# Weighting v in 16-bit with heads innermost: a ScalarE copy of v, a strided kv product, and a new instruction order in a fused attention and MLP kernel

## The chip, the cores and the metric

The kernel runs on one core of one Trainium2 chip. The metric is the device time of one execution in microseconds (us), median over runs. In the text PE is TensorE, ACT is ScalarE, DVE is VectorE, POOL is GpSimd, and SP is the engine that issues most DMA. SBUF and PSUM are the core's two on-chip memories; in this kernel PE's products land in PSUM, in banks of 512 32-bit columns. The granted clock is the share of its full clock that PE had, as the profile records it. "Span" is the length of the one profiled execution, some 2 us shorter than its time. "L773" is line 773 of that kernel's file; the same source statement has other line numbers in other kernels.

## The reference, cut to what matters

A pre-norm block: a layer norm, linear attention with a softmax feature map, then a second norm and a wide MLP (2048 tokens, 576 channels, 32 heads of 18, 4608 hidden).

```
q, k, v = split(layernorm(x) @ wqkv)            # 32 heads of 18
pk = einsum("bhsd,hdf->bhsf", k, w_phi)         # the same for q
phi_k = concat([softmax(pk), softmax(-pk)])
kv  = einsum("bhsf,bhsd->bhfd", phi_k, v)       # sum over the 2048 tokens
z   = sum of phi_k over tokens
o   = (phi_q . kv) / (phi_q . z)
h   = x + o @ wo
out = h + mlp(layernorm(layernorm(h)))
```

## The kernel before: the parts that matter here

The first 78 us (attention, first phase) walk over 16 tiles of 128 tokens. For tile t the kernel does K (PE: fused k projection; ACT: two exponentials), R (DVE: sums over each head's 18 features and their reciprocal), V (PE: v projection into PSUM banks 2 and 3), M (DVE: v times the reciprocal softmax sums, for both signs), and G (PE: the kv products of the exponentials with the weighted v, added up over the tiles). Q units (q projection with exponentials) fill PE where there is room. The v of a tile stays in PSUM until M has read it, because there is one pair of v banks.

```
def vx(t):                                   # weighted v: sign, head, value (value innermost)
    return vext[t % 2].rearrange("p (s h d) -> p s h d", s=2, h=H)

# M: 32-bit v out of PSUM times the 16-bit weight, broadcast over the 18 values
P.add("dve", lambda e: e.tensor_tensor(
    vx(t)[:, :, :, 0:DH],
    ps_all[:, 512 * VB:512 * VB + D].rearrange("p (h d) -> p h d", h=H).unsqueeze(1)
    .to_broadcast([128, 2, H, DH]),
    vx(t)[:, :, :, DH:DH + 1].to_broadcast([128, 2, H, DH]), ALU.mult), ...)

# G: for both signs and five groups of 7, 7, 7, 4, 7 heads
e.matmul(ps_all[:, col:col + 19 * nh], Ek[eb][:, ...],
         vext[vb][:, 608 * s + 19 * h0:608 * s + 19 * (h0 + nh)], ...)   # neighbouring columns

# kvr: after the last tile, kv out of PSUM times a 0/1 mask, two DVE operations
kvr[:, :, 0:25, 0:19] = ps_kv(512 * 5, [[512, 2], [19, 25], [1, 19]]) * mask25
kvr[:, :, 25:32, 0:19] = ps_kv(512 * 7, [[133, 2], [19, 7], [1, 19]]) * mask7
...
```

Every engine's instruction order is a list written out in the kernel (`PLAN`), one label per piece of work: K3, V2, M1, and so on. After kvr come the numerators N (PE) for the first two tiles, a serial chain over DVE, PE and POOL, and then the MLP, from about 95 us to the end.

The softmax here doesn't subtract the row's maximum and nothing guards it: scores larger than these inputs give would overflow.

## Time and profile before

| | before |
|---|---|
| time, median of 3 runs | 411.02 us |
| span | 408.5 us |
| first k projection starts | 11.79 us |
| first numerator product starts (PE timeline) | 77.80 us |
| first MLP product starts (PE timeline) | 95.18 us |
| PE busy from 13 to 78 us (windows) | 63.02 of 65.0 us |

The busy-time row of the page, and the first row of the chain that ended last (shares of the span by engine):

```profile
PE 398.3 (97%) x5000; PEld 288.5 (71%) x5000; DVE 180.7 (44%) x450; ACT 182.4 (45%) x422; POOL 93.7 (23%) x129
...
PE 87%; DMA 4%; DVE 4%; POOL 2%; ACT 1%; issue 1%; SPq 0%; DVEq 0%; POOLq 0%
```

PE bounds the kernel. The groups that the change touches, from 13 to 78 us (columns: line, engine, operation, output<-input, shapes, count | busy us, mean ns of one | idle time of the engine just before them and who ended it):

```profile
L786 DVE TENSOR_TENSOR RB<-ps_all,RB 128x1152 bf16<-128x1152 f32 x16 | 21.4, 1345 | 3.9 <-PE ps_all L763 3.9
L753 ACT ACTIVATE RB<-ps_all 128x576 bf16<-128x576 f32 x32 | 19.0, 647 | 8.0 <-PE ps_all L746 6.3 <-PE ps_all L801 1.7
L801 PE MATMUL ps_all<-RB 128*128 128x133 bf16 x128 | 11.4, 222 | 0.0
L1048 DVE TENSOR_TENSOR kvr<-ps_all,OTR 128x950 bf16<-128x950 f32 x1 | 1.2, 1151 | 1.0 <-PE ps_all L801 1.0
L1052 DVE TENSOR_TENSOR kvr<-ps_all,mask 128x266 bf16<-128x266 f32 x1 | 0.4, 428 | 0.0
```

L786 is the product M: 1.345 us for 1152 elements. L753 is the exponential of a 576-column tile out of PSUM: 0.647 us. L801 is a kv product (222 ns is the length of one; they overlap, and one starts 56 ns after the other). The waits of PE from 10 to 95 us (who waited <- for whom: us in total, times, longest):

```profile
PE ps_all L746 <- ACT tpn L486: 1.1, 1, 1.1
PE ps_all L564 <- DVE obuf L920: 0.6, 1, 0.6
PE ps_all L746 <- DVE RA L605: 0.5, 1, 0.5
PE ps_all L746 <- DMA yT<-ybuf: 0.5, 1, 0.5
...
```

No row shows PE waiting for M (L786), neither in its kv products (L801) nor in its v projection (L763). DVE has work to do, but it is not what PE waits for.

### The profile page before, as it was taken

How to read it: one execution, taken by the hardware profiler on the slowest of the kernel's cores; microseconds unless marked ns; L12 is line 12 of the kernel's file. 1: busy time of each engine (PE TensorE's matmuls, PEld its weight loads, DVE VectorE, ACT ScalarE, POOL GpSimd, SP SyncE). 2: the span in 40 equal slices, each digit the busy share in tenths (PEclk: the TensorE clock that was granted, in tenths of full speed). 3: DMA queues.
4: the chain of work that ended last, by engine and by line, in shares of the span. 5: the costliest groups of instructions: out<-in, count | busy, mean ns of one | idle time of the engine just before them, and what ended most of it. 6: DMA issues, size and time to landing. Idle time of an engine off the chain costs nothing.

```text
span 408.5 us, 11674 instructions
## 1 busy us (share of the span) xinstructions
PE 398.3 (97%) x5000; PEld 288.5 (71%) x5000; DVE 180.7 (44%) x450; ACT 182.4 (45%) x422; POOL 93.7 (23%) x129
## 2 busy tenths in 40 slices
PE   7998999989999999999999999999999999999996
PEld 4565666858965896599559956985697579658853
DVE  6997999786445125422442244234325412300000
ACT  5985856668840373046205700660175026404800
POOL 5578730022203203201220022002200220111000
PEclk9999999999999999999999999999999999999999
DMA  7699242495211100111110011001100120000000
GB/s 237 117 244 308 51 101 68 152 345 174 34 34 32 33 18 18 32 33 20 33 31 18 18 34 45 19 19 32 32 18 19 30 32 19 18 14 19 2 2 29
DMA packets 45595, 25.87 MB, mean 63 GB/s; under 512 B 32744, under 2 KB 44520, under 8 KB 45544
## 3 DMA queue, kind: packets, MB, share of 16 engines
q1 hardware_dynamic: 45400, 24.99, 24.1%
q8 instruction: 39, 0.64, 0.7%
q10 hardware_dynamic: 144, 0.15, 0.1%
q14 instruction: 12, 0.10, 0.1%
HBM read 15.13 MB, written 2.36 MB: 43 GB/s over the span
## 4 chain that ended last, share of the span: by engine, by line
PE 87%; DMA 4%; DVE 4%; POOL 2%; ACT 1%; issue 1%; SPq 0%; DVEq 0%; POOLq 0%
PE ps_all L1127 35%; PE ps_all L1195 35%; PE ps_all L952 4%; PE ps_all L763 3%; PE ps_all L831 3%; PE ps_all L746 3%; PE ps_all L852 2%; DMA yT<-ybuf 2%; PE ps_all L801 2%; DMA w2a<-in_A_wqkv_dram 1%; DMA x_all<-in_A_x_dram 1%; PE ps_all L615 1%; DVE x_all L972 1%; POOL ybuf L527 1%; DVE RA L605 0%
## 5 line engine op out<-in xcount | busy, mean ns | idle before, releaser
L1138 ACT ACTIVATE RA<-ps_all,b1T 128x256 bf16<-128x256 f32 x288 | 115.0, 479 | 176.9 <-PE ps_all L1127 162.1
L1127 PE MATMUL ps_all<-yT,w1sb 64*128 64x256 bf16 x2304 | 152.2, 269 | 0.0
L1127 PEld LDWEIGHTS ps_all<-yT,w1sb 64*128 64x128 bf16 x2304 | 135.0, 94 | 6.4
L1195 PE MATMUL ps_all<-w2a,RA 128*128 128x512 bf16 (+1 forms) x640 | 96.2, 286 | 0.0
L1127 PE MATMUL ps_all<-yT,w1t 64*128 64x256 bf16 x288 | 71.5, 270 | 0.0
L1195 PEld LDWEIGHTS ps_all<-w2a,RA 128*128 128x128 bf16 x640 | 45.8, 98 | 35.6 <-ACT RA L1138 1.5
L1195 PE MATMUL ps_all<-RB,RA 128*128 128x64 bf16 (+1 forms) x512 | 67.7, 286 | 0.0
L1204 DVE TENSOR_TENSOR WQ<-ps_all,tmpo 128x64 bf16<-128x64 f32 (+1 forms) x32 | 14.7, 458 | 101.5 <-PE ps_all L1195 89.1
L1195 PEld LDWEIGHTS ps_all<-RB,RA 128*128 128x128 bf16 x512 | 33.5, 98 | 32.3
L972 DVE SCALAR_TENSOR_TENSOR x_all<-ps_all,x_all 128x576 bf16<-128x576 f32 x16 | 12.1, 758 | 82.2 <-PE ps_all L952 82.1
L920 POOL TENSOR_TENSOR obuf<-tpn 128x576 bf16<-128x576 f32 x14 | 19.6, 1401 | 86.5 <-DVE tpn L915 76.4
L984 POOL TENSOR_TENSOR st<-st,neghalf 128x1 f32<-128x1 f32 x16 | 8.8, 552 | 133.3 <-DVE st L986 133.3
L837 ACT ACTIVATE Eq<-ps_all 128x512 bf16<-128x512 f32 (+1 forms) x48 | 25.3, 526 | 14.6 <-PE ps_all L831 13.4
L1201 POOL TENSOR_TENSOR tmpo<-x_all,b2bc 128x576 f32<-128x576 bf16 x16 | 20.4, 1274 | 43.5 <-DVE WQ L1204 43.5
L952 PE MATMUL ps_all<-wo_sb,OTR 64*128 64x288 bf16 x288 | 29.7, 283 | 0.2
L1127 PEld LDWEIGHTS ps_all<-yT,w1t 64*128 64x128 bf16 x288 | 26.3, 94 | 2.2 <-DVE WQ L1204 0.3
L831 PE MATMUL ps_all<-yT,WQ 128*128 128x256 bf16 x200 | 25.2, 273 | 0.2 <-ACT Eq L837 0.2
L746 PE MATMUL ps_all<-RA,yT 128*128 128x512 bf16 (+1 forms) x160 | 22.4, 286 | 2.5 <-ACT tpn L486 1.1
L786 DVE TENSOR_TENSOR RB<-ps_all,RB 128x1152 bf16<-128x1152 f32 x16 | 21.4, 1345 | 3.9 <-PE ps_all L763 3.9
L527 POOL TENSOR_SCALAR ybuf<-x_all,st 128x576 bf16<-128x576 bf16 x10 | 22.9, 2296 | 0.6 <-POOL st L514 0.6
L753 ACT ACTIVATE RB<-ps_all 128x576 bf16<-128x576 f32 x32 | 19.0, 647 | 8.0 <-PE ps_all L746 6.3
L763 PE MATMUL ps_all<-RB,yT 128*128 128x512 bf16 (+1 forms) x160 | 22.1, 286 | 0.0
(103 smaller groups left out, 317.0 us busy)
## 6 DMA issues: line engine op xcount, KB each, us to landing
w1sb<-in_B_w_dram SPq DMA_DIRECT2D x8, 576.0 KB, 6.9
w2a<-in_B_w_dram SPq DMA_DIRECT2D x4, 720.0 KB, 6.7
RB<-in_B_w_dram SPq DMA_DIRECT2D x2, 1152.0 KB, 7.6
out_dram<-WQ SPq DMA_DIRECT2D x16, 144.0 KB, 1.8
x_all<-in_A_x_dram SPq DMA_DIRECT2D x3, 576.0 KB, 4.9
w2a<-in_A_wqkv_dram SPq DMA_DIRECT2D x2, 288.0 KB, 5.4
RB<-in_A_wqkv_dram SPq DMA_DIRECT2D x1, 576.0 KB, 5.9
wo_sb<-in_A_wo_dram SPq DMA_DIRECT2D x1, 576.0 KB, 5.3
```

The lines of the kernel that those rows point to most:

```text
L527: P.add(eng, lambda e: e.tensor_scalar(ybuf[yb][:, 0:D], src, mean, rstd, ALU.subtract, ALU.mult), reads=[r_src, *r_st], writes=[res(f"ybu ...
L746: P.add("pe", lambda e, c=c, o=o, n=n: e.matmul(ps_all[:, 512 * KB + o:512 * KB + o + n], yT[:, c, sl * 128:(sl + 1) * 128], weffk[:, c, o ...
L763: P.add("pe", lambda e, c=c, o=o, n=n: e.matmul(ps_all[:, 512 * VB + o:512 * VB + o + n], yT[:, c, sl * 128:(sl + 1) * 128], wv[:, c, o:o ...
L786: P.add("dve", lambda e: e.tensor_tensor(vx(t)[:, :, :, 0:DH], ps_all[:, 512 * VB:512 * VB + D].rearrange("p (h d) -> p h d", h=H).unsquee ...
L831: P.add("pe", lambda e, i=i, c=c, h0=h0: e.matmul(ps_all[:, 512 * bk + RW * i:512 * bk + RW * i + RW], weffq[:, c, DH * h0:DH * h0 + 128], ...
L837: P.add("act", lambda e, s=s: e.activation(Eq[:, r, s, bs[0]:bs[0] + n, :], ps_all[:, 512 * bk:512 * bk + RW * n].rearrange("p (b t) -> p ...
L920: P.add(oeng, lambda e: e.tensor_tensor(obuf[ob][:, 0:D], tpn[:, 0, :], tpn[:, 1, :], ALU.add), reads=[res("tpn")], writes=[res(f"obuf{ob}")])
L952: P.add(lane, lambda e: e.matmul(ps_all[:, 512 * bk:512 * bk + DHF], oT[ob][h:h + 64, c, :], wo_sb[h:h + 64, c, o:o + DHF], start=first, s ...
L1127: P.add(lane, lambda e: e.matmul(ps_all[:, o:o + RW], lhs, yT[h:h + 64, c, ys], start=first, stop=not begin and i == 1 and c == 3, skip_gr ...
L1138: P.add("act", lambda e, m=m, o=o: e.activation(hmid[:, m, :], ps_all[:, o:o + RW], AF.Gelu_apprx_tanh, bias=b1T[:, m:m + 1]), reads=[res( ...
L1195: P.add("pe", lambda e, m=m, bk=bk, o=o, n=n: e.matmul(ps_all[:, 512 * bk:512 * bk + n], w2_lhs(m, j), w2_rhs(m, o, n), start=(m == 0), st ...
L1201: P.add("pool", lambda e: e.tensor_tensor(tmpo[:, :], x_all[:, t, :], b2bc[:, :], ALU.add), reads=[res("b2"), res(f"x{t}")], writes=[res(" ...
```

## The change

The intent: let M run on 16-bit operands in SBUF, both with a unit innermost step, so that DVE takes it at double rate. For that, heads become innermost in the weighted v, ACT copies v out of PSUM as bf16 with heads innermost (which also frees the v banks before M), the kv products read the weighted v at a step, and kvr turns the result round at the end. All engine orders, the split of work between the engines and the order of the first loads were set anew as well.

```
-WKL = [[0, 2], [2, 2]]
-STAT = "DDDADDAAAADADADA"     ... -WCOPY = "AAAAAA"
+STAT = "DDDDDDAADADAAADD"     ... +WCOPY = "AADDDA"
+VC = "1212121212121212"
 PLAN = { ... every list is new; act gains C0 ... C15 ... }

 def vx(t):
-    return vext[t % 2].rearrange("p (s h d) -> p s h d", s=2, h=H)
+    return vext[t % 2].rearrange("p (s d h) -> p s d h", s=2, h=H)
+
+def p1_vcopy(t, VB=VB):
+    ...
+    src = ps_all[:, 512 * VB:512 * VB + D]
+    dst = obuf[t % 2][:, 0:D]
+    if VC[t] == "1":
+        src, dst = src.rearrange("p (h d) -> p d h", h=H), dst.rearrange("p (d h) -> p d h", h=H)
+    else:
+        src, dst = src.rearrange("p (h d) -> p h d", h=H), dst.rearrange("p (d h) -> p h d", h=H)
+    P.add("act", lambda e: e.activation(dst, src, AF.Copy), ...)

 # M
-        vx(t)[:, :, :, 0:DH], ps_all[...] (h d) broadcast, vx(t)[:, :, :, DH:DH + 1] broadcast over d
+        vx(t)[:, :, 0:DH, :], obuf (d h) broadcast,        vx(t)[:, :, DH:DH + 1, :] broadcast over d

 # G
-                    vext[vb][:, 608 * s + 19 * h0:608 * s + 19 * (h0 + nh)],
+                    hap(RB, 9216, VO + 1216 * vb + 608 * s + h0, [[H, 19], [1, nh]]),

 # kvr: four operations instead of two; the first of them
+            (kvr[:, 0, 0:21, 0:19].rearrange("p (b h) d -> p b d h", b=3), ps_kv(512 * 5, [[133, 3], [7, 19], [1, 7]]),
+             mask25[:, 0:21, 0:1] ... .to_broadcast([128, 3, 19, 7]), (5,)),
 ...
```

## The prediction

> **What bounds the kernel now.** The profiled span is 408.5 us (median time 411.02). The chain of waits is 87% PE; the busy-time row gives PE 97%, DVE 44%, ACT 45%. By windows, from 95.3 us on (313 us, the feed-forward part) PE is busy 309.6 us; the change touches nothing there. From 37.5 to 78 us PE is busy without a gap. So only the first 37.5 us and a serial tail (78 to 95 us) can give time back.
>
> From the PE timeline (start to start: k projection 1.22 us a tile, v 1.22, kv 0.56, q units 1.09 or 0.55, weight products 1.7 us in all): from the first k (11.8 us) to the first numerator product (77.8 us) lie 66.0 us, and PE's own work is about 63.0. The 3.0 us of gaps are: 0.5 to 0.9 at 12 us (DVE copies of the fused k weight), 0.3 at 15 us and 0.3 at 17.9 us (k bank held by the exponentials on ACT), 1.2 at 32 us and 0.5 at 37 us (k projection 6 and 7 waiting for their DMA-transposed inputs, while DMA moves 295 GB/s). None is a wait for the v times weight product. Before, PE waits until 6.86 us for the k weights by DMA.
>
> **What changes.**
> - Removed from DVE: the product reads v from PSUM, 1.345 us x16 = 21.4 us. On 16-bit SBUF operands with heads innermost I expect the double rate that the Trainium skill, "VectorE: DVE Perf Modes", section "The perf-mode tier table", states for tensor_tensor (1x with any PSUM operand, 2x for bf16 in SBUF; no run here shows it yet). Estimate: the two kv mask operations (950 columns 1.151 us, 266 columns 0.428) give 1.06 ns a column, so 1.22 of 1.345 us is streaming; halved, 0.74 us, saving 9.7 us of DVE.
> - Added on ACT: 16 copies, 0.60 to 0.65 us each by the exponential of that shape (0.647): 10 us.
> - Rebalanced: two statistics (1.75 us of ACT, 1.15 of DVE) and three weight copies move from ACT to DVE. DVE ends about 5 us lighter, ACT about 4 us heavier.
> - The final kv mask: two DVE operations (1.15 + 0.43 us) become four (estimate 1.8 us), hidden by two q units (2.2 us).
> - kv products read the moving operand in runs of 4 or 7 columns at a 64-byte step. I expect 56 ns each, as now.
> - New orders: the k weights' DMA is issued 0.9 us earlier; bulk loads leave early transposes more room.
>
> **On the critical path.** The product itself is worth almost nothing, since PE doesn't wait for it. The gain is some 0.7 us at the start and half to two thirds of the 3.0 us of gaps.
>
> **Predicted time: 408.6 us**, 8 in 10 405.8 to 411.2. Faster by over 2%: 0.03; within 2%: 0.93; slower by over 2%: 0.04.
>
> **What would show it.** The product group near 0.74 us each; 16 ACT copies near 0.63 us; DVE busy down about 5 us, ACT up about 4; PE busy nearly unchanged; kv start-to-start still 0.56 us; first numerator product near 75.5 us instead of 77.8; the span from there on unchanged within 0.5 us.
>
> **What would make it wrong.** kv products slowed by the strided operand (doubled, they cost 9 us on a PE-bound stage, 2.2%); the product staying at single rate; ACT's added copies delaying the exponentials and so the k bank; feed-forward weights landing late.

## The result, and the profile after

The changed kernel took 423.27 us (median of 4 runs, 422.51 to 424.13) against 410.88 us for the kernel before (4 runs, that is one more than above): slower, ratio 1.0309, 95% interval 1.0262 to 1.0356. Here and below a ratio is the mean time of one kernel's fast runs over that of the other's of the same rounds, so it is not quite the ratio of the medians. All these runs are fast, that is none lies over 1.5% above the fastest of its kernel.

| | before | after |
|---|---|---|
| span | 408.5 us | 422.4 us |
| first k projection | 11.79 us | 10.76 us |
| first numerator product | 77.80 us | 89.56 us |
| first MLP product | 95.18 us | 109.35 us |
| end less first MLP product | 313.3 us | 313.1 us |

All the loss lies before the MLP: 11.8 us until the first numerator product although the start gained 1.0 us, and 2.4 us more between it and the MLP (19.79 us instead of 17.38). The busy row and the chain:

```profile
PE 402.5 (95%) x4999; PEld 293.4 (69%) x4999; DVE 179.2 (42%) x459; ACT 200.7 (48%) x427; POOL 97.6 (23%) x126
...
PE 83%; ACT 8%; DVE 5%; issue 1%; DMA 1%; POOL 0%; DVEq 0%; ACTq 0%
```

ACT rose by 18 us, not by 4, DVE fell by 1.5 us, not by 5, and ACT's share of the chain from 1% to 8%. The same groups, from 0 to 100 us:

```profile
L773 ACT ACTIVATE obuf<-ps_all 128x576 bf16<-128x576 f32 x16 | 26.8, 1675 | 3.2 <-DVE RB L797 1.6 <-PE ps_all L755 1.4
L797 DVE TENSOR_TENSOR RB<-obuf,RB 128x1152 bf16<-128x1152 bf16 x16 | 11.8, 749 | 7.0 <-ACT obuf L773 6.2 <-ACT tpn L478 0.5
L810 PE MATMUL ps_all<-RB 128*128 128x133 bf16 x128 | 13.7, 236 | 1.1 <-DVE RB L797 1.1
L1069 DVE TENSOR_TENSOR kvr<-ps_all,OTR 128x399 bf16<-128x399 f32 x2 | 3.8, 1882 | 0.6 <-PE ps_all L810 0.6
L1069 DVE TENSOR_TENSOR kvr<-ps_all,OTR 128x152 bf16<-128x152 f32 x1 | 0.8, 803 | 0.0
L1069 DVE TENSOR_TENSOR kvr<-ps_all,mask 128x266 bf16<-128x266 f32 x1 | 1.5, 1497 | 0.0
```

The product M (L797) did what was wanted: 0.749 us instead of 1.345. The kv products (L810) now start 71 ns after one another on average, not 56. But a copy (L773) takes 1.675 us on average, and a mask product of 399 elements takes 1.882 us where one of 950 had taken 1.151. An average hides two forms; the source view gives minimum, median and maximum of the copies (ns), and the ACT timeline from 15 us shows which is which (columns: start us, us, engine, line, operation):

```profile
L773 ACT ACTIVATE obuf<-ps_all x16: 645/1680/2707, 15.2 to 80.8; 128x576 bf16<-128x576 f32 x16
```

```profile
15.21 0.65 ACT L773 ACTIVATE obuf<-ps_all 128x576 bf16<-128x576 f32 x1
...
17.58 2.70 ACT L773 ACTIVATE obuf<-ps_all 128x576 bf16<-128x576 f32 x1 [0.31 <-PE ps_all L755]
...
22.46 0.66 ACT L773 ACTIVATE obuf<-ps_all 128x576 bf16<-128x576 f32 x1
```

Even tiles (form 1, stepped read of PSUM) take 0.65 us, odd tiles (form 2, stepped 2-byte write of SBUF) 2.70. That is 4.7 ns an element (2.70 us over 576), and the mask product's 1.882 us over 399 is 4.7 ns too, on another engine. What PE now waits for, from 10 to 110 us:

```profile
PE ps_all L755 <- ACT obuf L773: 6.9, 7, 1.5
PE ps_all L861 <- DVE kvr L1069: 3.2, 1, 3.2
PE ps_all L810 <- DVE RB L797: 1.1, 1, 1.1
...
```

The v projection waits seven times for a copy that still holds its bank, and the first numerator product waits 3.2 us for kvr. Then comes a sequel. The windows around that wait (columns: the stretch, its length, busy us and number of instructions of PE, PEld, DVE, ACT and POOL, granted PE clock, DMA share, GB/s):

```profile
84.80:89.60 4.80, 1.58 (x18) 1.21 (x16) 4.67 (x4) 1.65 (x3) 0.00 (x0) 0.96 0.62 187
89.60:92.20 2.60, 2.47 (x22) 2.23 (x23) 2.22 (x7) 0.00 (x0) 0.00 (x0) 0.50 1.09 369
92.20:96.00 3.80, 3.80 (x19) 2.71 (x18) 3.45 (x10) 1.35 (x3) 1.92 (x5) 0.50 1.04 402
96.00:109.30 13.30, 12.56 (x133) 8.96 (x130) 8.46 (x23) 10.14 (x20) 1.61 (x4) 1.00 0.72 236
```

After its idle stretch PE is granted half its clock until about 96 us. The Trainium skill, "TensorE: Matmul & The Clock Gate", section "Why this matters for your kernels", tells one to leave no gaps of more than about 3 us between bursts of matmuls or the clock halves; this trace agrees, with a wait of 3.22 us and a clock of 0.50 (e11 below has the half clock after two shorter waits).

### The profile page after: what moved, and what is told of

Same layout as the page of the kernel before. It is cut to its first block, busy times and chain, and to the rows that moved or that the text cites. A ratio compares the mean times of both kernels' runs of the same rounds, so it can differ in the third digit from the quotient of the medians.

```text
span 422.4 us, 11681 instructions
## 1 busy us (share of the span) xinstructions
PE 402.5 (95%) x4999; PEld 293.4 (69%) x4999; DVE 179.2 (42%) x459; ACT 200.7 (48%) x427; POOL 97.6 (23%) x126
## 4 chain that ended last, share of the span: by engine, by line
PE 83%; ACT 8%; DVE 5%; issue 1%; DMA 1%; POOL 0%; DVEq 0%; ACTq 0%
PE ps_all L1210 33%; PE ps_all L1142 33%; PE ps_all L961 5%; ACT obuf L773 5%; PE ps_all L755 3%; PE ps_all L840 3%; PE ps_all L861 2%; PE ps_all L738 2%; ACT Eq L846 2%; DVE kvr L1069 1%; PE ps_all L810 1%; ACT RB L745 1%; DMA x_all<-in_A_x_dram 1%; DVE sums L779 1%; DVE x_all L981 1%
## 5 line engine op out<-in xcount | busy, mean ns | idle before, releaser
L1142 PEld LDWEIGHTS ps_all<-yT,w1sb 64*128 64x128 bf16 x2304 | 136.9, 94 | 4.7
L519 POOL TENSOR_SCALAR ybuf<-x_all,st 128x576 bf16<-128x576 bf16 x12 | 28.1, 2348 | 1.0 <-POOL st L506 1.0
L773 ACT ACTIVATE obuf<-ps_all 128x576 bf16<-128x576 f32 x16 | 26.8, 1675 | 3.2 <-DVE RB L797 1.6
L840 PE MATMUL ps_all<-yT,WQ 128*128 128x256 bf16 x200 | 27.0, 287 | 0.4 <-ACT Eq L846 0.4
L779 DVE TENSOR_REDUCE sums<-RB 128x64 f32<-128x1152 bf16 x16 | 21.5, 1342 | 10.3 <-ACT RB L745 10.2
L840 PEld LDWEIGHTS ps_all<-yT,WQ 128*128 128x128 bf16 x200 | 19.4, 103 | 4.9 <-ACT Eq L846 0.6
```

The costliest lines, as they stand in the source:

```text
L519: P.add(eng, lambda e: e.tensor_scalar(ybuf[yb][:, 0:D], src, mean, rstd, ALU.subtract, ALU.mult), reads=[r_src, *r_st], writes=[res(f"ybu ...
L773: P.add("act", lambda e: e.activation(dst, src, AF.Copy), writes=[res(f"obuf{t % 2}")], banks=[bank[VB], bank[VB + 1]])
L779: P.add("dve", lambda e: e.tensor_reduce(sums[vb][:, :], Ek[eb][:, 0:1152].rearrange("p (h f) -> p h f", h=64), AX.X, ALU.add), reads=[res ...
L840: P.add("pe", lambda e, i=i, c=c, h0=h0: e.matmul(ps_all[:, 512 * bk + RW * i:512 * bk + RW * i + RW], weffq[:, c, DH * h0:DH * h0 + 128], ...
L1142: P.add(lane, lambda e: e.matmul(ps_all[:, o:o + RW], lhs, yT[h:h + 64, c, ys], start=first, stop=not begin and i == 1 and c == 3, skip_gr ...
```

## The experiments

Theory A: what is slow is the write of lone 2-byte elements far apart in SBUF; it holds up the v bank (copies of the odd tiles) and the numerators (kvr). Rivals: strided reads of PSUM are slow; the copies stand badly in ACT's order; the new order is itself slower; or the strided kv read is the loss. The first four runs shared a chip; the kernel before took 410.73 us there.

### e1_vc1: all copies in form 1

```
-VC = "1212121212121212"
+VC = "1111111111111111"
```

> The changed kernel with all 16 v copies in the form of the even tiles (read PSUM at a 72-byte step, write SBUF in unit steps). Theory A (a 2-byte write at a 64-byte step is what is slow): every copy 0.65 us, ACT about 16 us less busy, the waits of the v projection for the copies (6.9 us) gone, time about 416 to 417 us against 423.3. Rival B (ACT is late because the copies stand in its order before exponentials, whatever they cost): waits remain, time above 421. Rival C (strided PSUM reads are the slow ones): copies all go to 2.7 us and the time rises.

Measured: 415.08 us, ratio to before 1.0108 (1.0085 to 1.0131). The copies, and the longest waits of PE from 10 to 110 us:

```profile
L773 ACT ACTIVATE obuf<-ps_all x16: 645/650/658, 14.8 to 73.7; 128x576 bf16<-128x576 f32 x16
```

```profile
PE ps_all L861 <- DVE kvr L1069: 3.2, 1, 3.2
PE ps_all L738 <- DMA yT<-ybuf: 1.0, 2, 0.6
...
```

Every copy took 645 to 658 ns, the waits of the v projection for copies are gone from the waits of PE, and the first numerator product starts at 81.11 us, 8.45 us earlier than in the changed kernel. It gained a little more than expected. Rivals B and C fall: the copies kept their places in the order, and the strided PSUM read is as fast as a straight one (e8 has copies with no step at all, 0.650 us).

### e2_vc2: all copies in form 2

```
-VC = "1212121212121212"
+VC = "2222222222222222"
```

> The changed kernel with all 16 v copies in the form of the odd tiles (read PSUM in unit steps, write SBUF at a 64-byte step): the suspected cost doubled. Theory A: every copy 2.7 us, ACT about 16 us busier, ACT becomes the bound of the attention part, time 430 to 440 us. Rival C: all copies 0.65 us and the time falls to about 416.

Measured: 433.65 us (one run, state unknown). The copies:

```profile
L773 ACT ACTIVATE obuf<-ps_all x16: 2670/2697/2725, 14.9 to 91.8; 128x576 bf16<-128x576 f32 x16
```

PE waited 15.1 us in the v projection for them, and the first numerator product started at 100.53 us. Doubling the suspected cost about doubled the loss it causes (8.45 us taken away by e1, 10.97 us added here).

### e3_kvr: the mask products walk values innermost

```
-            (kvr[:, 0, 0:21, 0:19].rearrange("p (b h) d -> p b d h", b=3), ps_kv(512 * 5, [[133, 3], [7, 19], [1, 7]]),
-             mask25[:, 0:21, 0:1] ... .to_broadcast([128, 3, 19, 7]), (5,)),
+            (kvr[:, 0, 0:21, 0:19].rearrange("p (b h) d -> p b h d", b=3), ps_kv(512 * 5, [[133, 3], [1, 7], [7, 19]]),
+             mask25[:, 0:21, :].rearrange("p (b h) d -> p b h d", b=3), (5,)),
 ... the other three in the same way
```

> The changed kernel with the loops of the four final kv mask products turned round: head outside, value inside, so that SBUF is written in unit steps and PSUM is read at a 28-byte (or 16-byte) step. Theory A (write step): the four take about 1.7 us instead of 6.1, the 3.2 us wait of PE before the first numerator product goes, and the PE clock does not fall after it: 5 to 6.5 us faster than the changed kernel, about 417 us. Rival (the number of operations or the strided PSUM read is the cost): no change of their length.

Measured: 418.44 us, ratio 1.0192 (1.0172 to 1.0212), 4.8 us under the changed kernel's median, a little less than the 5 to 6.5 expected. The mask products in this run:

```profile
L1069 DVE TENSOR_TENSOR kvr<-ps_all,OTR 128x399 bf16<-128x399 f32 x2 | 1.2, 576 | 0.6 <-PE ps_all L810 0.6
L1069 DVE TENSOR_TENSOR kvr<-ps_all,mask 128x266 bf16<-128x266 f32 x1 | 0.4, 427 | 0.0
L1069 DVE TENSOR_TENSOR kvr<-ps_all,OTR 128x152 bf16<-128x152 f32 x1 | 0.3, 319 | 0.0
```

The same 399 elements take 576 ns instead of 1882, although PSUM is now read at a 28-byte step. So neither the number of operations nor the stepped PSUM read was the cost. The first numerator product starts at 86.39 us (3.17 earlier) and is not waited for; the clock stays at 1.00, and from there to the MLP it takes 17.39 us as before (103.78 less 86.39) instead of 19.79. The wait and the clock's fall went together in this run, so that the 2.4 us are the clock's is a reading of the windows: in the changed kernel PE was busy 6.3 of the 6.4 us from 89.6 to 96 us, at half clock.

### e4_vc1_kvr: both repairs

The edits of e1 and e3 together.

> Both repairs together (all copies and all mask products write in unit steps). Theory A with independent, additive costs: 11 to 13 us faster than the changed kernel, 410.5 to 412.5 us, that is within 1% of the kernel before; what is left against it is the slower kv product (72 ns against 56, 160 of them: 2.5 us) less what the new order gains. Rival (the new order is itself slower): stays above 415.

Measured: 410.74 us, ratio 1.0003 (0.9984 to 1.0022): as fast as the kernel before. The first MLP product starts at 95.58 us (before 95.18, changed 109.35). The three parts found one by one (8.45 + 3.17 + 2.40 = 14.0 us) match what the two repairs take away together (13.8 us). All of these come from one profiled run each; the medians differ by 12.5 us. The profiled run of the changed kernel is its slowest (424.13 us) and has mean clock 0.992, which two of its four runs have; the other two have 0.996, so the clock may have cost them less. The double repair settles the loss: without the lone 2-byte writes nothing of the net loss is left. What still stands against the early start and the quick product is next.

### e5_kvcontig: kv products read neighbouring columns (wrong values on purpose)

On top of e4:

```
-                    hap(RB, 9216, VO + 1216 * vb + 608 * s + h0, [[H, 19], [1, nh]]),
+                    vext[vb][:, 608 * s + 19 * h0:608 * s + 19 * (h0 + nh)],
```

> The doubly repaired kernel (time 410.7 us) with the kv products reading 133 (or 76) neighbouring columns instead of runs of 7 or 4 at a 64-byte step: wrong values on purpose, same sizes, same order. Theory (the strided moving operand costs 16 ns a product): kv start to start back to 0.56 us a tile from 0.71, 2 to 2.5 us faster, about 408.3 us. Rival (those 2.5 us are hidden elsewhere): within 0.5 us of 410.7.

This and the next three shared a chip, on which the kernel before took 409.41 us. Measured: 409.20 us, ratio 0.9981 (0.9954 to 1.0008), so about 0.2% or 0.9 us under e4 by the ratios; the two intervals overlap, so the times alone don't show that it is faster. The kv products of a tile go back from 0.71 to 0.56 us, 2.4 us in all, but the first numerator product starts only 0.82 us earlier (77.37 against 78.19). The rest is matched by other waits: PE's waits for the transposed inputs went from 1.4 to 1.8 us, and a wait of 0.9 us for a copy appeared. Start times in the trace show that the cost depends on the group: from one product to the next 66, 74 and 79 ns for the three first groups of 7 heads, which start 0, 14 and 28 bytes into a 64-byte row, against 57 to 63 ns when contiguous; the group of 4 heads, 42 bytes in, takes 67 instead of 37.5, and the last group of 7, 50 bytes in, 71 instead of 61.

### e6_order: the new order without the new layouts

The edit in shorthand:

```
 layouts, product, kv read and mask as in the kernel before; no copies (C labels dropped from act)
-dve: ... R1 M1 R2 R3 M2 M3 ... R10 R9 M9 M10 ... R12 R13 M12 R14 M14 M13 ...
+dve: ... R1 M1 R2 M2 R3 M3 ... R9 M9 R10 M10 ... R12 M12 R13 M13 R14 M14 ...
```

> Layouts, product, kv read and mask of the kernel before (no v copies at all), with the orders and engine assignments of the changed kernel; only the DVE order of sums and products is put back to alternate, since without copies the other order deadlocks. Theory (order and layout change are separate; my prediction gave the order 0.7 us at the start and more in the gaps): 1 to 2.5 us faster than before, 408 to 409.8 us. Rival (the new order only fits the new layouts): slower than before.

Measured: 430.46 us, ratio 1.0503 (1.0470 to 1.0535). The waits of PE:

```profile
PE ps_all L755 <- DVE RB L791: 16.9, 12, 4.1
...
```

Without a copy the v bank is held until M has read it, and this order asks for the next v much sooner. My expectation was wrong: the order is no separate gain. With this DVE order it only works with the copies; an order set anew for a kernel without copies was not tried.

### e7_nocopy: heads innermost, M reads PSUM

The edits of e3, no copies, and the DVE order of e6; M reads v from PSUM at a 72-byte step.

> Heads innermost kept and mask repaired, but no copies: the product reads v from PSUM at a 72-byte step in 32-bit. Theory (PE bounds this part, the product's speed is worth nothing): product about 1.35 us instead of 0.78, DVE some 9 us busier, ACT 10 us lighter, time within 1 us of the doubly repaired kernel's 410.7. Rival (the double rate product, or freeing the v bank early, is worth time): slower than 412.

Measured: 431.74 us, ratio 1.0549 (1.0518 to 1.0580). M took 1.346 us as expected, but PE waited 15.3 us in the v projection for it. The rival holds: in this order the copies and the short M together are worth some 22 us (1.0549 against e4's 1.0003). Part of that is the clock: after a wait of 4.08 us it is 0.50 for 6.8 us. The run doesn't tell how much is the copy and how much M's length; the next gives an idea.

### e8_copy_hd: the copies, but values innermost

The edit in shorthand:

```
 VC = "3333333333333333"   # v copied straight, no step on either side
-vx(t): (s d h)            +vx(t): (s h d), kv read and mask as in the kernel before
-M: obuf (d h) times the weight row, heads innermost
+M: obuf (h d) times the weight, broadcast innermost (step 0)
```

> The changed kernel's order with the copies, but v copied straight (no step on either side), and weighted v, kv read and mask in the layouts of the kernel before; the product reads 16-bit v with the weight broadcast innermost (step 0). Theory: product stays at single rate, 1.25 to 1.35 us, yet the time equals the one with contiguous kv reads, 408 to 409 us, since only the kv read matters. Rival (single rate product now costs): slower than 410.7.

Measured: 414.16 us, ratio 1.0109 (1.0088 to 1.0130). M and PE's waits:

```profile
L791 DVE TENSOR_TENSOR RB<-obuf,RB 128x1152 bf16<-128x1152 bf16 x16 | 21.5, 1358 | 1.1 <-ACT RB L745 0.5
```

```profile
PE ps_all L738 <- DMA yT<-ybuf: 2.3, 4, 0.9
PE ps_all L805 <- DVE RB L791: 2.0, 2, 1.1
PE ps_all L738 <- ACT tpn L480: 1.6, 1, 1.6
...
```

M has 16-bit operands in SBUF as in e5 but takes 1.358 us instead of e5's 0.792; its weight is broadcast innermost (step 0). The Trainium skill, "Advanced Engine Details and Errata", section "2x-1p Requirements", asks for a unit step in the innermost dimension besides 16-bit types; the pair of 0.749 us and 1.358 us agrees. (M's output differs too, runs of 18 elements in rows of 19 instead of runs of 32; no run parts the two.) Against e5, which also reads kv in neighbouring columns, this kernel is 1.3% slower (1.0109 over 0.9981), some 5 us. So in the new order M's speed is worth about 5 us: the kv products wait 2.0 us for it; that the rest is other DVE work coming late was not traced. My expectation that it is worth nothing was wrong for this order. The copies took 0.650 us here without any step in PSUM, the same as form 1 with one.

### e9_probe: the disputed costs by themselves

The kernel of e4 with copies from PSUM to SBUF and products appended after the last output tile, each with another step.

> The doubly repaired kernel with measuring instructions after the last output tile: ACT and DVE copies from PSUM to 16-bit SBUF with element steps 1, 2, 4, 8, 16, 32 and with runs of 2 and 4 at step 32; the same to 32-bit SBUF; and products with 12 repeats whose moving operand has such steps. Theory A (the cost is that of writing a lone 2-byte element): the slow rate of about 4.6 ns an element shows at some step and above on both engines alike, runs of 2 or 4 elements shrink it, and 32-bit writes at a step cost much less. Rival (the cost is only that of the step in bytes): 32-bit writes at 64 bytes are as slow as 16-bit ones. For PE: single elements at a 64-byte step cost more than the 14-byte runs (about 72 ns for 133 columns), contiguous ones 56 ns.

The durations, one instruction each for ACT and DVE (the state of this single run is unknown, and no times are compared across runs); element counts differ a little so that the rows can be told apart.

| write to SBUF | elements | ACT ns | DVE ns |
|---|---|---|---|
| 2-byte, neighbouring | 288 | 446 | 449 |
| 2-byte, 4 bytes apart | 280 | 486 | 476 |
| 2-byte, 8 bytes apart | 272 | 780 | 770 |
| 2-byte, 16 bytes apart | 264 | 1352 | 1345 |
| 2-byte, 32 bytes apart | 256 | 1262 | 1252 |
| 2-byte, 64 bytes apart | 248 | 1261 | 1237 |
| pairs of 2-byte, 64 bytes apart | 240 | 373 | 407 |
| fours of 2-byte, 64 bytes apart | 232 | 364 | 399 |
| 4-byte, neighbouring | 288 | 411 | 458 |
| 4-byte, 8 bytes apart | 280 | 421 | 450 |
| 4-byte, 16 bytes apart | 270 | 684 | 631 |
| 4-byte, 64 bytes apart | 72 | 290 | 278 |

Two of these rows as the groups view prints them:

```profile
L1257 ACT ACTIVATE Eq<-ps_all 128x248 bf16<-128x248 f32 x1 | 1.3, 1261 | 0.0
L1257 ACT ACTIVATE Eq<-ps_all 128x240 bf16<-128x240 f32 x1 | 0.4, 373 | 0.0
```

Lone 2-byte elements cost nearly twice as much an element at an 8-byte step and about three times as much from a 16-byte step on, alike on both engines; two elements side by side at the same 64-byte step cost nothing extra; 4-byte writes at 16 bytes cost half as much as 2-byte ones. Theory A holds and the plain rival (the step in bytes alone) falls. The Trainium skill, "Advanced Engine Details and Errata", section "SBUF Cachelines", speaks of 16-byte lines in which at least two hits are needed for full rate; the free pairs agree. But at 8 bytes two elements fall into each 16 bytes, and still 272 took 780 ns against 446 for 288 neighbours: here two hits did not bring the full rate. Why the lone write is so slow inside the memory no run shows.

For PE, the time from start to start of 12 equal products (start times in the trace): 58 ns for 133 neighbouring columns, 62 ns for 18 runs of 7 at 64 bytes that start at the row's beginning, 110 ns for 64 pairs, 220 ns for 130 lone columns, all at 64 bytes, and 233 ns for 131 lone columns at 16 bytes. But 132 lone columns 4 bytes apart took 59 ns, 17 runs of 7 at 16 bytes 59, and 31 runs of 4 at 64 bytes 103. So a step is not dear by itself, and the cost is no fixed sum a run either (31 runs of 4 took nearly as long as 64 pairs); no rule comes out of these eight.

### e10, e11, e12: the repaired change in the old order, and the early loads alone

e10 puts the repaired change (copies in form 1, mask of e3) into the kernel before, with its order and assignments; each copy goes into ACT's list behind the exponentials of the next tile (K1 C0, K2 C1, ...). e11 is the kernel before with only the first loads moved:

```
-act: lx0 exp S3 ...                               sp: lx1 lx2 lwk0 lwk2 lphi0 lwk4 lphi2 lphi1 lwv4 lx3 lwv ...
+act: lx0 lphi0 lphi1 lphi2 exp S3 ...             sp: lwk0 lwk2 lwk4 lx1 lx2 lwv4 lx3 lwv ...
```

e12 has both. The kernel before took 410.13 us on this chip.

> The change alone, repaired (all copies and mask products write in unit steps), in the order and assignments of the kernel before; each copy is put into ACT's order right behind the exponentials of the next tile. Theory (in the order before, PE never waits for the product, so its speed is worth nothing there, while the strided kv reads cost up to 2.5 us and ACT gets 10 us more): 1 to 3 us slower than before, 411 to 413.5. Rival (freeing the v bank early and the fast product help in any order): faster than before.

Measured: 413.73 us, ratio 1.0083 (1.0061 to 1.0105); first numerator product at 81.88 us. The change alone loses in the old order, by 3.4 us by the ratio, a little more than expected. 2.4 us of kv products is one part; PE's waits give no single other culprit, and this trace lacks 11 of PE's records in the stretch, so they can't be summed.

> The kernel before with nothing but the first loads reordered as in the changed kernel (k weights first on the SP queue, tile 0 of x and the feature weights on the ACT queue). The changed kernel starts its first k projection at 10.8 us instead of 11.8. Theory: about 0.7 us faster than before (409 to 410), less if tile 1 then comes late. Rival (the start is bound by something else): no change.

Measured: 411.80 us, ratio 1.0036 (1.0012 to 1.0061). A miss: the early k weights bring tile 1 late. In the old order DVE takes tile 1's statistics before it normalises tile 0, so it waits 1.83 us for the load, PE waits 1.79 us for tile 0's rows and then 1.91 us for a weight copy on DVE, and the first k projection gets past its first product at 13.3 us instead of 12.7. After these two waits the clock is 0.50 from 11.70 to 15.11 us, although neither is as long as 3 us. The changed kernel's DVE list has tile 0's rows first (S0 Y0 S1, not S0 S1 Y0), so these loads too belong to their order.

> Both of these together. If the two act apart, its time is that of the repaired change in the old order less what the loads alone gain.

Measured: 415.25 us, ratio 1.0124 (1.0100 to 1.0148). The two losses add (0.83% and 0.36% make 1.19%).

Taken together, e4 (1.0003) and e10 (1.0083) are the same repaired change in the new and the old order: the new order, with its assignments and loads, is worth 0.8% to it, about 3.3 us. No version beat the kernel before beyond the noise; the nearest, e5, gives wrong values.

## Why the prediction was wrong, point by point

I predicted 408.6 us (405.8 to 411.2) and 93% for "within 2%". It was 423.27 us, 3.1% slower.

- **"Added on ACT: 16 copies, 0.60 to 0.65 us each by the exponential of that shape (0.647): 10 us."** This step failed. The exponential writes neighbouring elements; half of the copies write lone 2-byte elements 64 bytes apart and took 2.70 us. The sum was 26.8 us, the bank of v was held, and taking that away brought the first numerator product 8.45 us forward (e1). I had read the line of the diff with the two forms and costed both by shape alone.
- **"The final kv mask: ... four (estimate 1.8 us), hidden by two q units (2.2 us)."** This step failed for the same reason: 6.1 us summed over the four, 3.2 us of it seen by PE. With unit steps the four sum to 1.9 us and are nearly hidden (e3), so the estimate was right for what I had taken them to be. The halved clock after that wait, some 2.4 us, was nowhere in my sum.
- **"kv products ... I expect 56 ns each, as now."** Wrong in size: 71 ns on average, 2.4 us in all. It cost 0.8 us in the end by the traces of e4 and e5, within the noise of their times. I listed it as the main danger, and it was the smallest of the three.
- **The product near 0.74 us.** Right: 0.749. The Trainium skill, "VectorE: DVE Perf Modes", section "The perf-mode tier table", gives tensor_tensor twice the rate for bf16 in SBUF than with any PSUM operand, and this trace agrees (1.345 to 0.749 us).
- **"The product itself is worth almost nothing, since PE doesn't wait for it."** Right for the order before: there no wait of PE names it. Wrong for the new order, where single rate goes with about 5 us (e8).
- **"The gain is some 0.7 us at the start and half to two thirds of the 3.0 us of gaps."** This step failed too. The first k projection did start about 1 us earlier. But even in e5, with the slow copies, masks and kv reads all gone, it is 66.8 us from there to the first numerator product (10.57 to 77.37) against 66.0 before: none of the gaps came back. And I took the order for something added on top. It is built on the copies: without them it is 5% slower than before (e6), and with the repaired change it recovers 3.3 us (e4 against e10), just what the change costs.
- **"The span from there on unchanged within 0.5 us."** Right for the MLP (313.3 and 313.1 us), wrong for the serial tail because of the clock.

What stays open: why e10 loses 3.4 us when its kv products account for at most 2.4; and whether another layout of the groups would make the repaired change pay (the last group lies within one 16-byte stretch and still took 71 ns). In e5 the whole kv read was worth about 1 us.

## What to carry to other kernels

Cost a copy or product by the step of its innermost write as well as by its shape: when a 16-bit layout has to be turned round between PSUM and SBUF, put the step on the PSUM read and keep the SBUF write in neighbouring elements, or at least in pairs. Look at minimum and maximum of a group, not only at its mean, wherever a kernel has two forms of one operation. A hand-set instruction order and the buffers' lifetimes it was made for form one change: neither is to be costed, nor taken over, without the other.

## What the Trainium skill lacked or had wrong

- "Advanced Engine Details and Errata", section "SBUF Cachelines", names a penalty for touching another line with each access but gives no size and does not speak of writes; "Vector Engine (DVE) Microarchitecture Reference", section "Measured stream behaviour on trn2", has no lone 2-byte writes either. Here: lone 2-byte writes at steps of 16 bytes or more took 1237 to 1352 ns for 248 to 264 elements on DVE and ACT, against about 447 ns for 288 neighbouring ones; pairs at 64 bytes took 373 and 407 ns for 240. The page's two hits on a line did not bring the full rate here: 272 elements 8 bytes apart, two to 16 bytes, took 780 and 770 ns.
- "ScalarE: Activation LUTs", section "What ACT_TABLE_LOAD costs", has an ACTIVATE with immediate scale and bias at 186 ns + 0.833 ns an element for every function, so 666 ns at 576 (an estimate by that page). Measured: 650 ns with neighbouring writes, 2697 ns (median of e2) with lone 2-byte writes 64 bytes apart. The page has no word on the output's step.
- "Advanced Engine Details and Errata", section "PSUM Cachelines", warns that non-contiguous patterns slow matmuls down. A reader may extend that to ACT and DVE reading PSUM; here an ACT copy reading at a 72-byte step took 650 ns, as one without a step did, and DVE's product took 1.346 us at a 72-byte step against 1.345 in order.
- No page that I found gives the cost of a stepped moving operand for PE: at a 64-byte step 220 ns for 130 lone columns, 110 ns for 64 pairs, 62 ns for 126 columns in aligned runs of 7, 58 ns for 133 contiguous ones, 59 ns for 132 lone ones at a 4-byte step; runs that start 14 or 28 bytes into the row took 74 and 79 ns for 133.
